# A state-space mixer with an MLP gate on one core: rows of the second half are stored early and gated products added in DRAM by accumulating DMAs

## The chip, the core and the metric

The kernel runs on one core of a Trainium2 chip. The core has five engines that run side by side, each in its own order: PE (matrix products), DVE (elementwise work on vectors), ACT (functions of one operand), POOL (some elementwise work early on, near the end an issuer of DMAs alone) and SP (an issuer of DMAs alone). ACT can issue DMAs too. The metric is the device time in microseconds (us) of one execution. Before the change it is 1081.44 us, the median of three runs (1080.97 to 1081.83).

## What is computed

The input `u` has 2048 tokens of 576 features. Each token is normalized; a long convolution along the tokens gives `s`, a two-layer network on each token gives `g`, and the output is the input plus their product:

```
xn  = layernorm(u)
s   = ssm_conv(xn)                      # a convolution of length 2048 per feature, by transforms
h   = gelu(xn @ w1 + b1)                # 576 -> 4608
g   = silu(h @ w2 + b2)                 # 4608 -> 576
out = u + s * g                         # float32
```

## The kernel before

**Tiling.** Tokens are cut into 16 tiles of 128. The tiles 0 to 7 are called the first half here, 8 to 15 the second. The hidden width of 4608 is cut into 12 groups of 384. A *slot* is one group for one block of four tiles: layer 1 (`layer1`, L519) makes three blocks of 128 hidden rows for 512 tokens, `hidden` turns them into a high part `hh` and a low part `hl` (L552, L555, L558), and layer 2 (`layer2`, L577) multiplies them with `w2` for four tiles, called j = 0 to 3. Each product is formed from three matmuls (high by high, low by high, high by low). After each tile of a slot DVE adds the PSUM result to the running sum `acc` (`add`, L585). There are 48 slots, PE works through them without a break, and the convolution's work is threaded in between.

**The end.** The last two slots finish tiles 8 to 11 and 12 to 15. As each tile's `acc` is complete, `finish` (L644) is called for it. For tiles 8 to 11 the gate is formed with tanh: ACT makes tanh(z/2) (L653), DVE multiplies `s` by z (L660) and by (1 + tanh) (L664). For tiles 12 to 15 it is formed with silu on ACT (L653) and one product on DVE (L658). Then `total` adds the product to the input row (L668) and stores the tile's sum with two DMAs of 64 rows each (L671), on SP; for tiles 14 and 15 the second of the two goes through ACT. The last tile, 15, is done in two halves of 288 columns: layer 2 writes its second half to another PSUM buffer (`cv`) so that the first half can be finished while PE still works.

**Where the rows come from.** `last_x` (L630) loads the input rows of tiles 8 to 15 on SP into freed table memory (named `w` and `v` in the trace), `last_s` (L636) loads their `s` into the freed buffer `A2` (named `A`). Both happen well ahead of the end. `combine_load` and `combine` (L613, L621) do the same for tiles 0 to 7 on POOL's queue, from stored gates: three loads, two DVE operations (L624, L625) and stores (L628). Their last set, tiles 6 and 7 in columns 384 to 576, falls between the two last slots. The buffers `row` (four of them) are shared by these loads and by ACT's gate (L653).

**What sets the order.** A planner (`Order`) keeps a modelled clock for each engine and traces the steps of many work lines in the order that its costs give; the traced order is then pinned on each engine. `finish` returns such steps, `need` names what a step must wait for in that model. Semaphore waits between engines follow from the data: an instruction waits for whoever wrote what it reads or reads what it overwrites. An engine that waits holds up what is queued behind it. A DMA also waits, on its issuing engine, for the DMA eight places earlier of its kind.

Of the kernel before, what the change touches and what calls it, by code (L numbers as in the profile page):

```python
# [13 lines left out]
OP = mybir.AluOpType  # L14
# [3 lines left out]
L, D, N, F = 2048, 576, 128, 4608  # L18
# [24 lines left out]
def dve(n):  # L43
    return 0.075 + 0.00104 * n
# [163 lines left out]
def step(eng, dur, fn, need=(), mark=None, cv=0, at=0.0, late=0.0, tbl=None, by=1e9):  # L208
    return dict(eng=eng, dur=dur, fn=fn, need=tuple(need), mark=mark, cv=cv, at=at, late=late, tbl=tbl, by=by)
# [3 lines left out]
def mixer_kernel(ctx, tc, u, log_a_real, a_imag, c_real, c_imag, log_dt, d_skip, w1, b1, w2, b2,  # L213
                 f1, f2, g2, g1, tvals, ident, out, parts=("mlp", "s4d")):
    nc = tc.nc
# [9 lines left out]
    def dram(ap_of, offset, ap):  # L225
        return bass.AP(tensor=ap_of.tensor, offset=ap_of.offset + offset, ap=ap)
# [97 lines left out]
    acc = sb.tile([P, 8, D], F32, name="acc")  # L324
# [283 lines left out]
    XS = {}  # L608

    def rows_at(t, b, c0, c1):  # L610
        return [dram(t, (b + 16 * y) * D + c0, [[32 * D, 64], [1, c1 - c0]]) for y in range(2)]
# [24 lines left out]
    def last_s(k):  # L636

        m = A2F[:, k * D:(k + 1) * D]
        nc.sync.dma_start(m, s_s[:, 8 + k, :])
        XS[8 + k] = (TM[k], m)  # L640

    TM = []

    def finish(b, c0, c1, silu, end):  # L644

        c = slice(c0, c1)
        z = acc[:, b - 8, c]
        n = c1 - c0
        T = []

        def act_z():
            T.append(sb.tile([P, D], F32, name="row", bufs=NROW)[:, c])
            nc.scalar.activation(T[0], z, AF.Silu if silu else AF.Tanh, scale=1.0 if silu else 0.5)  # L653

        def mul():
            s = XS[b][1][:, c]
            if silu:
                nc.vector.scalar_tensor_tensor(s, s, 2.0, T[0], op0=OP.mult, op1=OP.mult)  # L658
            else:
                nc.vector.tensor_mul(s, s, z)  # L660

        def mul2():
            s = XS[b][1][:, c]
            nc.vector.scalar_tensor_tensor(s, T[0], 1.0, s, op0=OP.add, op1=OP.mult)  # L664

        def total():
            x, s = XS[b]
            nc.vector.tensor_add(x[:, c], x[:, c], s[:, c])  # L668
            for y, o in enumerate(rows_at(out, b, c.start, c.stop)):
                queue = nc.scalar if end and y else nc.sync  # L670
                queue.dma_start(o, x[64 * y:64 * y + 64, c])  # L671
        st = [step("ACT", act(n), act_z, tbl="silu" if silu else "gelu"), step("DVE", dve(n), mul)]
        if not silu:
            st.append(step("DVE", dve(n), mul2))
        return st + [step("DVE", dve(n), total)]


    def params():
# [426 lines left out]
    NSLOT = 4 * NG  # L1105
    od = Order(tc, nc)
    od.pinned = True
    el, wl2, wl, nl2, pl, pl2, pl3, pl4, pl5, nl, ml, ml2, xl, wx, c3, c2, c1, kl, tl, sl, vl, gl, fl, f2l = [od.line() for _ in range(24)]
# [260 lines left out]
    for k in range(4):  # L1369
        gl["steps"].append(step("POOL", 5.0, lambda k=k: part.update({k: load_g2(k)}), mark=("g2", k),  # L1370
                                need=[("g2c", k - 1)] if k else []))
# [112 lines left out]
    for slot in range(NSLOT):  # L1484
        turn[0] = slot + 1
        n, g, tb = SEQ[slot]
        change = slot + 1 < NSLOT and SEQ[slot + 1][0] != n
        final = slot >= NSLOT - 2
        for pos in range(NPOS):
            if pos < G:  # L1490
                need = wmark(n, 1) + [("x", tb)]
                if pos == 0:
                    if slot in (mid, mid + 1):
                        x_ready(tb)
                    od.force(lambda: all(m in od.marks for m in need))

                    if slot in (3, 2 * NG + 1):
                        od.marks["x", tb] -= 2.3
                cell = []
                od.unit(lambda: cell.extend([layer1(g, tb, pos)] if slot else first_layer1(pos)),  # L1500
                        L1 if slot else L1 * (22, 6, 14)[pos] / 14, need)
                look_ahead(pos)
                for k, (a, b, c) in enumerate(cell, pos + 1 - len(cell)):
                    by = hidden_by(pos, k)
                    od.urgent.append((od.t["PE"], [step("ACT", 0.62, a, tbl="gelu", by=by[0]),
                                                   step("ACT", act(TB), b, by=by[1]),
                                                   step("DVE", dve(TB), c, mark=("h", slot, k), by=by[2])]))
                od.advance(od.t["PE"])
                if pos == G - 1 and change:
                    weigh_in(1)  # L1510
            else:
                j, terms, last, hid = l2_terms(pos - G)
                need = [wmark(n, 2)[i] for i in hid] + [("h", slot, i) for i in hid]
                if pos == G:

                    pe_turns()
                od.force(lambda: all(m in od.marks for m in need))
                if max(od.marks[m] for m in need) > od.t["PE"] + 0.3:
                    pe_turns(any_time=True)
                cell = []  # L1520
                halves = slot == NSLOT - 1 and j == 3
                od.unit(lambda: cell.append(layer2(g, tb, j, terms, last, halves)), LEN[pos], need)
                look_ahead(pos)
                if last or halves:
                    add = cell[0]
                    dh, k = (terms[0][1], 1) if halves else (0, 2)
                    done = ("acc", slot, j, dh)
                    chain = [step("DVE", dve(288 * k), lambda: add(dh, k), mark=done, by=add_by(pos, j))]
                    if final:
                        b = 8 + 4 * tb + j  # L1530
                        x = el if slot < NSLOT - 1 else od.line()
                        st = finish(b, dh * 288, (dh + k) * 288, slot == NSLOT - 1, slot == NSLOT - 1 and j > 1)
                        st[0]["need"] = (done, ("s8", b - 8))
                        x["steps"] += st
                    elif slot in GATE:
                        for d in range(2):
                            one, two = gate_store(4 * tb + j, d)
                            by = od.t["PE"] + 5.0
                            chain += [step("ACT", act(288), one, tbl="gelu", by=by), step("DVE", dve(288), two, by=by)]
                    od.urgent.append((od.t["PE"], chain))  # L1540
                if pos == NPOS - 1 and change:
                    weigh_in(2)
            for f in LATER.get((slot, pos), ()):
                f()
            od.advance(od.t["PE"])
            pe_turns(all_lines=pos in (0, 1, G + 1, G + 3, G + 5, NPOS - 1))
# [55 lines left out]
```

## Time and profile before

| | us |
|---|---|
| median of three runs | 1081.44 |
| profiled execution, its own time | 1081.68 |
| its span, first to last instruction | 1079.9 |
| PE busy (99% of the span) | 1070.8 |
| DVE busy (88%) | 955.2 |
| ACT busy (61%) | 662.2 |
| POOL busy (20%) | 211.0 |

Times in the views count from the span's start. The span is 1.8 us shorter than the execution's own time; that part lies outside of what the profile shows. The granted clock of PE is 0.998 over the span. A row of the timeline gives the start, the duration, the engine and its line, the operation, what it writes and reads, and in brackets the engine's idle time before it with what ended it. "Landing" of a DMA is the time from the start of its issue until its completion reaches the semaphore.

### The profile page before, as it was taken

The page shows a single profiled execution, that of the slowest core. Times are in us where ns is not written, and L with a number is a line of the kernel's source. Part 1 is how long each engine was busy: PE and PEld are TensorE (multiplying, and loading weights), DVE is VectorE, ACT ScalarE, POOL GpSimd, SP SyncE. Part 2 cuts the span into 40 slices and gives each one's busy share as a digit, 9 for nine tenths or more (in the row PEclk, how much of TensorE's full clock was granted, in tenths as well). Part 3 has the DMA queues.
Part 4 walks back from the last instruction along what each step waited for, and adds up shares of the span by engine and source line. Part 5 has one row for each costly group of instructions (what it writes and reads, how often), then busy time and mean ns, then how long its engine had stood idle before and what let it go on. Part 6 is the DMA issues. An engine that isn't in the chain of part 4 may idle for free.

```text
span 1079.9 us, 27247 instructions
## 1 busy us (share of the span) xinstructions
PE 1070.8 (99%) x11471; PEld 932.4 (86%) x11471; DVE 955.2 (88%) x1535; ACT 662.2 (61%) x985; POOL 211.0 (20%) x304
## 2 busy tenths in 40 slices
PE   9999999999999999999999999999999999999997
PEld 7989899888888888888888887898888888888896
DVE  7789878999999999999999999999999997668367
ACT  6656768877658575686657657566667655234233
POOL 5669433111100020000200002000200013011231
PEclk9999999999999999999999999999999999999999
DMA  7885456643224141457322244133322436343434
GB/s 233 236 261 184 145 180 213 197 109 131 65 76 120 30 128 52 107 148 147 89 62 77 65 85 118 32 107 51 103 59 85 125 60 229 98 132 98 128 117 121
DMA packets 138570, 129.71 MB, mean 120 GB/s; under 512 B 88636, under 2 KB 109216, under 8 KB 137424
## 3 DMA queue, kind: packets, MB, share of 16 engines
q1 hardware_dynamic: 121792, 78.31, 26.8%
q0 software_dynamic: 15904, 48.70, 14.6%
q8 instruction: 90, 1.47, 0.6%
q10 hardware_dynamic: 752, 0.97, 0.3%
q14 instruction: 32, 0.26, 0.1%
HBM read 98.50 MB, written 35.19 MB: 124 GB/s over the span
## 4 chain that ended last, share of the span: by engine, by line
PE 96%; DVE 3%; issue 1%; ACT 0%; POOL 0%; ACTq 0%; DVEq 0%; POOLq 0%
PE mxb L577 21%; PE mxa L577 21%; PE mxa L519 21%; PE mxb L519 20%; PE cv L881 3%; PE cv L991 3%; PE cv L1044 2%; PE cv L953 2%; PE cv L1071 1%; PE mxa L1132 1%; DVE w2l L496 0%; PE mxa L534 0%; DVE pr L720 0%; DVE hl L558 0%; DVE A L658 0%
## 5 line engine op out<-in xcount | busy, mean ns | idle before, releaser
L577 PE MATMUL mxa<-w2h,hh 128*128 128x288 f32 x573 | 171.3, 299 | 0.3 <-DVE acc L585 0.3
L577 PE MATMUL mxb<-w2h,hh 128*128 128x288 f32 x576 | 171.6, 298 | 0.0
L577 PE MATMUL mxb<-w2h,hl 128*128 128x288 f32 x576 | 170.2, 296 | 0.0
L577 PE MATMUL mxb<-w2l,hh 128*128 128x288 f32 x576 | 169.5, 294 | 0.0
L577 PE MATMUL mxa<-w2h,hl 128*128 128x288 f32 x573 | 169.4, 296 | 0.2 <-DVE hl L558 0.2
L577 PE MATMUL mxa<-w2l,hh 128*128 128x288 f32 x573 | 168.7, 294 | 0.0
L558 DVE TENSOR_TENSOR hl<-h,hh 128x512 fp32r<-128x512 f32 x144 | 99.2, 690 | 65.2 <-ACT hh L555 64.7
L552 ACT ACTIVATE h<-mxa,b1t 128x512 f32<-128x512 f32 x73 | 50.3, 690 | 120.8 <-PE mxa L519 119.8
L781 POOL DMA_DIRECT2D par<-par_s x36 | 27.4, 762 | 480.4 <-DVE mg L824 436.4
L577 PEld LDWEIGHTS mxa<-w2h,hh 128*128 128x128 f32 x573 | 107.6, 188 | 9.8 <-issue 4.7
L577 PEld LDWEIGHTS mxb<-w2h,hh 128*128 128x128 f32 x576 | 108.1, 188 | 7.7 <-issue 3.0
L577 PEld LDWEIGHTS mxb<-w2l,hh 128*128 128x128 f32 x576 | 108.1, 188 | 0.6
L577 PEld LDWEIGHTS mxb<-w2h,hl 128*128 128x128 f32 x576 | 108.1, 188 | 0.4 <-DVE hl L558 0.2
L577 PEld LDWEIGHTS mxa<-w2h,hl 128*128 128x128 f32 x573 | 107.5, 188 | 0.6 <-DVE hl L558 0.6
L577 PEld LDWEIGHTS mxa<-w2l,hh 128*128 128x128 f32 x573 | 107.6, 188 | 0.5
L552 ACT ACTIVATE h<-mxb,b1t 128x512 f32<-128x512 f32 x71 | 49.0, 690 | 74.0 <-PE mxb L519 73.3
L555 ACT ACTIVATE hh<-h 128x512 fp32r<-128x512 f32 x144 | 91.2, 634 | 4.2
L585 DVE TENSOR_TENSOR acc<-mxa,acc 128x576 f32<-128x576 f32 x88 | 65.7, 746 | 21.3 <-PE mxa L577 20.8
L519 PE MATMUL mxa<-XH,w1h 128*128 128x512 f32 x284 | 78.9, 400 | 0.0
L519 PE MATMUL mxb<-XH,w1h 128*128 128x512 f32 x280 | 77.5, 398 | 0.0
L519 PE MATMUL mxa<-XL,w1h 128*128 128x512 f32 x284 | 76.2, 390 | 0.0
L519 PE MATMUL mxa<-XH,w1l 128*128 128x512 f32 x284 | 76.0, 389 | 0.0
(239 smaller groups left out, 2450.9 us busy)
## 6 DMA issues: line engine op xcount, KB each, us to landing
raw<-in_B_w_dram SPq DMA_DIRECT2D x75, 288.0 KB, 3.3
raw<-in_B_w_dram SPq DMA_DIRECT2D x100, 192.0 KB, 3.4
par_s<-A POOLq DMA_DIRECT2D x8, 1080.0 KB, 5.2
par<-par_s POOLq DMA_DIRECT2D x36, 240.0 KB, 3.4
f2t<-f2q SPq DMA_DIRECT2D x24, 256.0 KB, 3.5
raw<-in_B_w_dram SPq DMA_DIRECT2D x50, 96.0 KB, 3.6
u_s<-in_A_u_dram POOLq DMA_DIRECT2D x16, 288.0 KB, 4.8
xc<-xn_s SPq DMA_DIRECT2D x48, 96.0 KB, 3.8
```

Source lines behind the costliest of these rows:

```text
L519: nc.tensor.matmul(q, a, b, start=j == 0, stop=j == len(ops) - 1)
L552: nc.scalar.activation(t, q, AF.Gelu_apprx_tanh, bias=b1t[:, g * G + i:g * G + i + 1], scale=1.0)
L555: LAST[0] = nc.scalar.activation(hh[:, i], t, AF.Copy)
L558: nc.vector.tensor_sub(hl[:, i], t, hh[:, i].bitcast(F32))
L577: nc.tensor.matmul(q[:, dh, :288], a[:, i, c], b[:, i, d], start=i == 0 and k == 0, stop=i == G - 1 and k == 2)
L585: nc.vector.tensor_add(o, q[:, dh:dh + n, :288], b if first else o)
L781: nc.gpsimd.dma_start(PAR[b].rearrange("p (g i) k -> p g (i k)", g=4), dram(par_s, (b // 6 * CH + b % 6 * 4) * NPAR, [[D * NPAR, P], [24 * ...
L881: nc.tensor.matmul(q[32 * g:32 * g + 32, i // 2, i % 2 * 64:i % 2 * 64 + 64], U[:, ri, 4 * g + i, :], v[:, ri, 4 * g + i, :], start=ri == ...
L953: nc.tensor.matmul(Q1ST[i, x][g // 2][64 * f:64 * f + 64, g % 2].rearrange(order), f1t[r].rearrange("p s k -> p (s k)"), rhs(r, f), start= ...
L991: nc.tensor.matmul(Q[i][32 * q:32 * q + 32, f, 2 * ri:2 * ri + 2], m[r, 4 * i + q, 32 * ri:32 * ri + 32], A2[r, 4 * p + 2 * i + q // 2, :, ...
L1044: nc.tensor.matmul(QI[q // 2][64 * f:64 * f + 64, q % 2, i], MAT["g2t", p + i // 2][r, i % 2, ri], YS[p + i // 2][0][r, i % 2, ri, f], sta ...
L1071: nc.tensor.matmul(Q[f][32 * e:32 * e + 32, t], g1t[r], A2[r, k:k + 2, 1].rearrange("p i d r -> p i r d"), start=True, stop=True, skip_gro ...
```

## The change

```diff
--- before.py
+++ after.py
@@ -638,6 +638,9 @@
         m = A2F[:, k * D:(k + 1) * D]
         nc.sync.dma_start(m, s_s[:, 8 + k, :])
         XS[8 + k] = (TM[k], m)
+        if k < 7:
+            for y, o in enumerate(rows_at(out, 8 + k, 0, D)):
+                nc.sync.dma_start(o, TM[k][64 * y:64 * y + 64])
 
     TM = []
 
@@ -652,27 +655,34 @@
             T.append(sb.tile([P, D], F32, name="row", bufs=NROW)[:, c])
             nc.scalar.activation(T[0], z, AF.Silu if silu else AF.Tanh, scale=1.0 if silu else 0.5)
 
+        def product(a, k, op, b2):
+            x, s = XS[b]
+            o = s[:, c] if end else x[:, c]
+            nc.vector.scalar_tensor_tensor(o, a, k, b2, op0=op, op1=OP.mult)
+            if not end:
+                for y, r in enumerate(rows_at(out, b, c0, c1)):
+                    nc.gpsimd.dma_start(r, o[64 * y:64 * y + 64], accum_op=OP.add)
+
         def mul():
             s = XS[b][1][:, c]
             if silu:
-                nc.vector.scalar_tensor_tensor(s, s, 2.0, T[0], op0=OP.mult, op1=OP.mult)
+                product(s, 2.0, OP.mult, T[0])
             else:
                 nc.vector.tensor_mul(s, s, z)
 
         def mul2():
-            s = XS[b][1][:, c]
-            nc.vector.scalar_tensor_tensor(s, T[0], 1.0, s, op0=OP.add, op1=OP.mult)
+            product(T[0], 1.0, OP.add, XS[b][1][:, c])
 
         def total():
             x, s = XS[b]
             nc.vector.tensor_add(x[:, c], x[:, c], s[:, c])
             for y, o in enumerate(rows_at(out, b, c.start, c.stop)):
-                queue = nc.scalar if end and y else nc.sync
+                queue = nc.scalar if c1 == D and y else nc.sync
                 queue.dma_start(o, x[64 * y:64 * y + 64, c])
         st = [step("ACT", act(n), act_z, tbl="silu" if silu else "gelu"), step("DVE", dve(n), mul)]
         if not silu:
             st.append(step("DVE", dve(n), mul2))
-        return st + [step("DVE", dve(n), total)]
+        return st + [step("DVE", dve(n), total)] * end
 
 
     def params():
@@ -1529,8 +1539,10 @@
                     if final:
                         b = 8 + 4 * tb + j
                         x = el if slot < NSLOT - 1 else od.line()
-                        st = finish(b, dh * 288, (dh + k) * 288, slot == NSLOT - 1, slot == NSLOT - 1 and j > 1)
+                        st = finish(b, dh * 288, (dh + k) * 288, slot == NSLOT - 1, slot == NSLOT - 1 and j == 3)
                         st[0]["need"] = (done, ("s8", b - 8))
+                        if halves and not dh:
+                            st[1]["need"] = (("acc", slot, j, 1),)
                         x["steps"] += st
                     elif slot in GATE:
                         for d in range(2):
```

For tiles 8 to 14 the input rows, once loaded, are stored to `out` at once, with two DMAs per tile on SP that directly follow the load of that tile's `s` in SP's order. The gate's last product is then written over the loaded row tile and added to `out` by two DMAs per tile that POOL issues with an accumulating operation; the DVE sum and the SP stores (or SP and ACT) at the end go away for these seven tiles. The last tile keeps its sums and plain stores, and only the very last of its four stores is on ACT. In the model, the first half's product of the last tile also waits for the second half's `acc`.

At the program's end, DVE stood as follows before. `acc<-mxb_12986`, `acc<-mxa_13013` and `acc<-cv_13027` are the sums of tile 14 and of the two halves of tile 15; `w` and `v` are the input rows, `row` the gates, `A2` is `s`.

```order
L668 TENSOR_TENSOR w_11310<-w_11310,A2_81 128x576
L658 SCALAR_TENSOR_TENSOR A2_81<-A2_81,row_12997 128x576
L585 TENSOR_TENSOR acc_87<-mxb_12986,acc_87 128x576
L668 TENSOR_TENSOR w_11310<-w_11310,A2_81 128x576
L585 TENSOR_TENSOR acc_87<-mxa_13013,acc_87 128x288
L658 SCALAR_TENSOR_TENSOR A2_81<-A2_81,row_13037 128x576
L585 TENSOR_TENSOR acc_87<-cv_13027,acc_87 128x288
L668 TENSOR_TENSOR v_11311<-v_11311,A2_81 128x576
L658 SCALAR_TENSOR_TENSOR A2_81<-A2_81,row_13040 128x288
L668 TENSOR_TENSOR v_11311<-v_11311,A2_81 128x288
L658 SCALAR_TENSOR_TENSOR A2_81<-A2_81,row_13046 128x288
L668 TENSOR_TENSOR v_11311<-v_11311,A2_81 128x288
```

And with the change, where `acc<-mxb_12996`, `acc<-mxa_13024` and `acc<-cv_13037` are the same three sums:

```order
L585 TENSOR_TENSOR acc_87<-mxa_12961,acc_87 128x576
L661 SCALAR_TENSOR_TENSOR w_11310<-A2_81,row_12993 128x576
L661 SCALAR_TENSOR_TENSOR w_11310<-A2_81,row_13009 128x576
L585 TENSOR_TENSOR acc_87<-mxb_12996,acc_87 128x576
L585 TENSOR_TENSOR acc_87<-mxa_13024,acc_87 128x288
L661 SCALAR_TENSOR_TENSOR v_11311<-A2_81,row_13034 128x576
L585 TENSOR_TENSOR acc_87<-cv_13037,acc_87 128x288
L661 SCALAR_TENSOR_TENSOR A2_81<-A2_81,row_13050 128x288
L678 TENSOR_TENSOR v_11311<-v_11311,A2_81 128x288
L661 SCALAR_TENSOR_TENSOR A2_81<-A2_81,row_13054 128x288
L678 TENSOR_TENSOR v_11311<-v_11311,A2_81 128x288
```

The full-width sums of tiles 12 to 14 (L668, 576 wide) are gone, and `acc<-cv` of the last half stands directly behind tile 14's product, ahead of the first half's product.

ACT's end before, with the gates of tiles 12, 13, 14 and of tile 15's halves:

```order
L653 ACTIVATE row_12983<-acc_87 128x576
L653 ACTIVATE row_12997<-acc_87 128x576
L653 ACTIVATE row_13037<-acc_87 128x576
L653 ACTIVATE row_13040<-acc_87 128x288
L671 DMA out_0_dram<-v_11311 64x576
L653 ACTIVATE row_13046<-acc_87 128x288
L671 DMA out_0_dram<-v_11311 64x288 x2
```

With the change:

```order
L656 ACTIVATE row_12993<-acc_87 128x576
L656 ACTIVATE row_13009<-acc_87 128x576
L656 ACTIVATE row_13034<-acc_87 128x576
L656 ACTIVATE row_13050<-acc_87 128x288
L656 ACTIVATE row_13054<-acc_87 128x288
L681 DMA out_0_dram<-v_11311 64x288
```

The DMA that stood between the two half gates of tile 15 is gone, and only one store is left.

POOL's end before, from the second to last set of first-half stores on:

```order
L628 DMA out_0_dram<-row_12711 64x192 x6
L616 DMA row_12873<-u_s_65 128x2x192
L617 DMA row_12874<-s_s_64 128x2x192
L618 DMA row_12875<-g_s_68 128x2x192
L628 DMA out_0_dram<-row_12873 64x192 x4
```

With the change, L664 being the accumulating DMAs, `w_11309` and `w_11310` holding tiles 8 to 10 and 11 to 13, `v_11311` tiles 14 and 15:

```order
L628 DMA out_0_dram<-row_12725 64x192 x6
L664 DMA out_0_dram<-w_11309 64x576 x4
L616 DMA row_12890<-u_s_65 128x2x192
L617 DMA row_12891<-s_s_64 128x2x192
L618 DMA row_12892<-g_s_68 128x2x192
L664 DMA out_0_dram<-w_11309 64x576 x2
L664 DMA out_0_dram<-w_11310 64x576 x2
L628 DMA out_0_dram<-row_12890 64x192 x4
L664 DMA out_0_dram<-w_11310 64x576 x4
L664 DMA out_0_dram<-v_11311 64x576 x2
```

Four accumulating DMAs (tiles 8 and 9) now stand ahead of the loads for the last first-half set, four (tiles 10 and 11) ahead of that set's stores, and six (tiles 12 to 14) behind them at the queue's end. On SP, each load of `s` (L639) for tiles 8 to 14 is now followed by two stores of rows, among the last three loads of `w2` (L459), which before had one load of `s` between them; the order on PE is the same.

## The prediction

> **What bounds the kernel now.** I read the page's busy times first, then its chain of work, then the stretches at the end, then the timelines of the engines there.
>
> ```profile
> PE 1070.8 (99%) x11471; PEld 932.4 (86%) x11471; DVE 955.2 (88%) x1535; ACT 662.2 (61%) x985; POOL 211.0 (20%) x304
> PE 96%; DVE 3%; issue 1%; ACT 0%; POOL 0%; ACTq 0%; DVEq 0%; POOLq 0%
> 1060.00:1066.00 6.00, 6.00 (x38) 5.46 (x37) 4.10 (x8) 3.93 (x5) 0.00 (x0) 1.00 0.42 98
> 1072.80:1079.90 7.10, 0.00 (x0) 0.00 (x0) 3.29 (x7) 0.83 (x2) 0.00 (x0) 0.71 0.49 125
> ```
>
> PE is busy for 99% of the span and makes 96% of the chain. The stretch from 1060 to 1066 (columns: length, then busy us of PE, weight load, DVE, ACT, POOL, clock, DMA) shows it full in the last slot as well. The change leaves PE's instructions and their order alone, so as long as nobody makes PE wait, it can only alter what comes behind PE's last matmul, the 7.1 us of the last row. PE's last matmul and DVE's work around it:
>
> ```profile
> 1072.48 0.29 PE L577 MATMUL cv<-w2h,hl 128*128 128x288 f32 x1
> ...
> 1068.73 0.75 DVE L658 SCALAR_TENSOR_TENSOR A<-A,row 128x576 f32<-128x576 f32 x1
> 1069.52 0.76 DVE L668 TENSOR_TENSOR w<-w,A 128x576 f32<-128x576 f32 x1
> 1070.19 0.75 DVE L658 SCALAR_TENSOR_TENSOR A<-A,row 128x576 f32<-128x576 f32 x1
> 1070.86 0.75 DVE L585 TENSOR_TENSOR acc<-mxb,acc 128x576 f32<-128x576 f32 x1
> 1071.53 0.75 DVE L668 TENSOR_TENSOR w<-w,A 128x576 f32<-128x576 f32 x1
> 1072.20 0.45 DVE L585 TENSOR_TENSOR acc<-mxa,acc 128x288 f32<-128x288 f32 x1
> 1072.56 0.75 DVE L658 SCALAR_TENSOR_TENSOR A<-A,row 128x576 f32<-128x576 f32 x1
> 1073.23 0.45 DVE L585 TENSOR_TENSOR acc<-cv,acc 128x288 f32<-128x288 f32 x1
> 1073.60 0.75 DVE L668 TENSOR_TENSOR v<-v,A 128x576 f32<-128x576 f32 x1
> 1074.26 0.45 DVE L658 SCALAR_TENSOR_TENSOR A<-A,row 128x288 f32<-128x288 f32 x1
> 1074.75 0.46 DVE L668 TENSOR_TENSOR v<-v,A 128x288 f32<-128x288 f32 x1
> 1075.60 0.46 DVE L658 SCALAR_TENSOR_TENSOR A<-A,row 128x288 f32<-128x288 f32 x1 [0.39 <-ACT row L653]
> 1076.09 0.46 DVE L668 TENSOR_TENSOR v<-v,A 128x288 f32<-128x288 f32 x1
> ```
>
> PE ends at 1072.48 + 0.29 = 1072.77, but DVE adds the last half (`acc<-cv`) only at 1073.23: it is 0.46 behind, with two full-width totals (L668 at 1069.52 and 1071.53) in its way. Then ACT:
>
> ```profile
> 1068.85 0.69 ACT L653 ACTIVATE row<-acc 128x576 f32<-128x576 f32 x1 [0.91 <-DVE acc L585]
> ...
> 1074.38 0.54 ACTq L671 DMA_DIRECT2D out_dram<-v  x1
> 1075.12 0.45 ACT L653 ACTIVATE row<-acc 128x288 f32<-128x288 f32 x1 [1.93 <-DVE A L658]
> ```
>
> The last gate could start at 1073.23 + 0.45 = 1073.68. It starts at 1075.12, since ACT's queue holds tile 14's store ahead of it, and that waits for the total that DVE ends at 1074.35. So the tail holds two losses: 0.46 us on DVE and 1.44 us on ACT. Behind them come the last product, the last total (its end 1076.55) and the stores:
>
> ```profile
> L671 ACTq DMA_DIRECT2D out_dram<-v x1: 498/498/498, 1076.6 to 1076.6; - x1
> DMA to landing us min/median/max: 2.0/2.1/2.2
> ...
> L1598 SPq DRAIN  x3: 7/7/7, 1079.1 to 1079.4; - x3
> ```
>
> The last two stores are issued at 1076.6 on SP and ACT and land 2.0 and 2.2 later, the later one at 1078.8; SP, which waits for all DMAs at the end, lets go at 1079.1, and the span ends at 1079.9. From last landing to the end: 1.1 us.
>
> **The tail rebuilt, step by step.** Durations are those of the rows above. Independent neighbours on DVE start 0.67 apart (1070.19 to 1070.86) at full width and 0.37 (1073.23 to 1073.60) after a half; dependent halves start 0.49 apart (1075.60 to 1076.09). An engine takes up another's result 0.03 to 0.06 later. Tile 12's product stays at 1068.73. Without its total, tile 13's product starts at 1069.6 in place of 1070.19, when its gate (1068.85 + 0.69) is ready. Tile 14's sum starts when PE is done with it, about 1070.45; its gate on ACT runs 1071.23 to 1071.92; the first half's sum comes with PE at 1071.62, its gate ends at 1072.55; tile 14's product runs 1072.05 to 1072.80. The last sum now starts with PE's end, 1072.81, ends at 1073.26; the last gate, with no DMA in ACT's queue ahead, runs 1073.29 to 1073.74. Meanwhile DVE makes the first half's product at 1073.18 and its total at 1073.67. The last product starts at 1074.04, the last total at 1074.53, ending 1074.99 where it was 1076.55: **1.56 us earlier**.
>
> Not all of it arrives. The first half's two stores are now both on SP:
>
> ```profile
> 1072.31 1.11 SPq L671 DMA_DIRECT2D out_dram<-w  x2
> ```
>
> A pair holds SP for 1.11 us. From 1074.16 it ends at 1075.3, so SP's last store starts about 1075.35, not 1075.02; it lands 2.0 later at 1077.35 (ACT's lands 2.2 after 1075.02, or 2.5 at worst: not later than 1077.5). Before, SP's landed at 1078.6. The gain on this path is **1.2 us**. All seven removed totals (seven times 0.75) otherwise free only DVE time that waits for PE anyway, as the chain's 96% says: nothing beyond the two in the tail.
>
> **The added accumulating DMAs.** POOL takes up a DVE result late:
>
> ```profile
> 1065.88 0.56 DVE L625 TENSOR_TENSOR row<-row 128x384 f32<-128x384 f32 x1
> ...
> 1066.73 2.13 POOL L628 DMA_DIRECT2D out_dram<-row  x4 [10.92 <-DVE row L625]
> ```
>
> 0.30 us after DVE's end (1066.43), and 0.53 us for each DMA of 64 rows. Tile 12's pair then issues from 1069.8, tile 13's from 1070.9 to 1072.0, tile 14's at 1073.1 and 1073.65, ending 1074.2. No row shows an accumulating DMA, which has to read `out` as well as write it. The nearest:
>
> ```profile
> g_s<-acc POOLq DMA_DIRECT2D x8, 288.0 KB, 2.4
> out_dram<-row POOLq DMA_DIRECT2D x16, 48.0 KB, 1.9
> u_s<-in_A_u_dram POOLq DMA_DIRECT2D x16, 288.0 KB, 4.8
> row<-u_s POOLq DMA_DIRECT2D x9, 192.0 KB, 3.4
> ```
>
> A plain store of POOL, 288 KB, lands after 2.4 us: the lower bound for these 144 KB. A copy of 288 KB within DRAM, which reads and writes there, takes 4.8: the upper bound. A load of 192 KB takes 3.4, about 1 us above a store, and I take that 1 us for the read: 2.4 + 1.0 = 3.4, so the last one lands at 1077.05, ahead of SP's 1077.35: hidden by the last tile's own chain. At 4.8 it lands at 1078.45 and, with 1.1 us behind it, ends the span at 1079.55: the gain shrinks to 0.35.
>
> The Trainium skill speaks to this (Collectives: The Full Stack, "The bandwidth ceiling: the fold count and why AG ≠ RS ≠ AR"): an add inside the DMA engine costs a second read, so it moves at half the rate, and nothing for the add itself. With the fit of DMA: Bandwidth & Descriptors ("Anatomy of one DMA — SWDGE (gpsimd) path"), 2.0 us plus bytes over 436 GB/s, 147,456 bytes read twice would land after an estimated 2.7 us; no run here shows it yet, and by it the sum would stay and the case in which the landing holds the end would lose its ground.
>
> POOL also has a closing step of its own:
>
> ```profile
> L1598 POOLq DRAIN  x3: 46/103/3731, 1068.1 to 1079.6; - x3
> ```
>
> It ends 3.73 after 1068.08, at 1071.8: 2.95 after POOL's last issue ended (1066.73 + 2.13 = 1068.86). Counted so, it now ends at 1077.15, free. Its DMAs had landed by about 1070.2 (1.9 after the last issue's start); if it follows the landing by 1.65, it ends at 1078.7 and releases the end 0.4 before the old 1079.1. I take the first, since ACT's queue shows no such tie; the second goes to a rival.
>
> **Earlier work that is moved.** The fourteen early stores cost SP issue time among the last weight loads:
>
> ```profile
> 1017.04 2.69 SPq L639 DMA_DIRECT2D A<-s_s  x5
> 1028.22 0.81 SPq L459 DMA_DIRECT2D raw<-in_B_w_dram  x2
> 1030.28 0.33 SPq L459 DMA_DIRECT2D raw<-in_B_w_dram  x1
> 1034.70 1.84 ACT L499 ACTIVATE w2h<-raw 128x576 fp32r<-128x576 f32 x3 [6.09 <-PE mxa L577]
> ```
>
> Ten of them, with five loads, sit between 1017.04 and the load at 1028.22, which is released by DVE: about 15 times 0.55, or 8.3 us of 11.2, with some waiting for the DMA eight earlier. One pair (1.11) then precedes the third `w2` load, which moves from 1030.28 to about 1030.8, lands some 3.3 later at 1034.1, and is needed for the third of ACT's splits, from 1035.9: 1.8 us of cover. On POOL, four accumulating DMAs precede the loads for the last first-half set:
>
> ```profile
> 1053.08 0.73 POOL L616 DMA_DIRECT2D row<-u_s  x1
> 1055.09 0.72 POOL L618 DMA_DIRECT2D row<-g_s  x1 [0.56 <-issue]
> 1065.29 0.55 DVE L624 TENSOR_TENSOR row<-row 128x384 f32<-128x384 f32 x1
> ```
>
> Tile 9's product is ready near 1054, so the loads issue from 1055.2 instead of 1053.08; the last lands near 1057 + 4 = 1061, and DVE wants it at 1065.3: 4 us of cover. ACT's gates of tiles 8 to 11 now stand together ahead of the next gelu, which may come one gate (0.69 us) later at worst; two more layer-1 blocks of PE stand before its result is wanted. These edits cost nothing; without the covers each would show as PE idle, one for one.
>
> **The sum.** Span 1079.9 - 1.2 = 1078.7, and 1081.68 - 1.2 = 1080.5 for the profiled execution, which lies 0.24 above the median. On the median's scale: 1081.44 - 1.2 = 1080.24, rounded to **1080.3 us**.
>
> **The rivals.**
> - *POOL's end holds the end*: the accumulating landing at 4.8, or the closing step tied to it. The lower bound of 0.35 to 0.4 us gained, up to a wash: 1081.0 to 1081.8. For it: the read of DRAM is unmeasured, and the closing step's length is unexplained. Against it: the landing has 0.3 us to spare at 3.4.
> - *Slower, by POOL's issue*: an accumulating DMA that holds POOL longer than 0.53. Six follow tile 12's product from 1069.8, so the last starts at 1069.8 + 5t and lands 3.4 later; it passes the old last landing (1078.8) at t = 1.1. At t = 1.5 the end is 1.9 us later (1083.3), at t = 2 it is 4.4 later (1085.8). For it: nothing shows such a DMA. Against it: 64 rows cost 0.53 and the 256 rows of the load at 1053.08 cost 0.73, so the number of rows hardly matters.
> - *PE is made to wait* in the last two slots, by slow accumulating DMAs ahead of the first-half loads or by traffic on the weights: beyond the 4 or 1.8 us of cover, each microsecond adds one; 2 to 5 us, 1083 to 1086.
> - *The tail doesn't shorten*, because ACT's last gate waits for the first-half stores that free its `row` buffer. They issue by 1068.86 and land near 1070.2, 3 us ahead of 1073.3: only with POOL held up, which is the second rival.
>
> **How the numbers follow.** The forecast gets 0.66, the first rival 0.18, the second 0.11, the third 0.05; the last has no share of its own. The forecast's own range is 1079.7 to 1081.0 (the runs of before spread by 0.4 either way). The range to give goes from 1079.7 to 1083.0: it takes in the first rival and the milder part of the second. A change of 0.2%, 2.16 us, is about what a measurement of this kernel can tell from none. A gain of that size would have to come from more than the two losses in the tail, whose 1.9 us are already an upper bound: 0.03. Slower by that needs t near 1.5 or a held PE: 0.11. Within 0.2%: 0.86.
>
> **What would show it.** `acc<-cv` within 0.1 us of PE's end; the last gate directly behind it; the last total ending 2.2 us after PE (before 3.8); seven fewer L668; accumulating issues of 0.53 and landings between 2.4 and 4.8; POOL's closing step over before SP's. Wrong it would be by idle time of PE after 1015, by POOL issues over 1 us each, or by a last landing that is POOL's.

## The result and the profile after

The change makes the kernel **slower**: 1083.34 us (median of 19 runs, 1082.58 to 1084.61) against 1081.41 us for the kernel before in the same rounds (19 runs, 1080.83 to 1082.35). The ratio is 1.0019 with a 95% interval of 1.0012 to 1.0026, so the loss is 1.3 to 2.8 us, where a gain of about 1.2 was forecast.

The profiled execution of the change took 1084.61 us, the highest of its runs, with a span of 1082.8. PE's last matmul ends 0.68 us later than before, at 1073.16 + 0.29 = 1073.45. That shift stands almost whole (0.60) at DVE's first sum already, 26 us into the span and ahead of everything the change moves (every engine's order is the same up to 1018 us), and PE has no wait that it had not before; it belongs to the execution and not to the change. All tails are therefore compared from PE's end on. The tail was 7.13 us (1072.77 to 1079.9) and is now **9.38** (1073.45 to 1082.83): 2.25 more, about the difference of the medians (1.93).

The end of the kernel after, in the timelines of PE, DVE and ACT:

```profile
1073.16 0.29 PE L577 MATMUL cv<-w2h,hl 128*128 128x288 f32 x1
...
1072.67 0.75 DVE L661 SCALAR_TENSOR_TENSOR v<-A,row 128x576 f32<-128x576 f32 x1
1073.49 0.46 DVE L585 TENSOR_TENSOR acc<-cv,acc 128x288 f32<-128x288 f32 x1
...
1075.21 0.46 DVE L678 TENSOR_TENSOR v<-v,A 128x288 f32<-128x288 f32 x1
...
1073.98 0.44 ACT L656 ACTIVATE row<-acc 128x288 f32<-128x288 f32 x1 [0.68 <-DVE acc L585]
```

The last sum follows PE by 0.04 us (0.46 before), the last gate starts 0.53 behind PE's end (2.35 before), and the last total ends 2.22 behind it (3.77 before). The arithmetic is done 1.55 us earlier, as forecast. What follows is DMAs. The stretches behind PE's end (length, busy us of PE, weight load, DVE, ACT, POOL, then clock, share of the DMA engines and GB/s):

```profile
1073.40:1076.00 2.60, 0.05 (x1) 0.00 (x0) 2.13 (x6) 0.44 (x1) 2.16 (x3) 0.88 0.98 133
1076.00:1080.40 4.40, 0.00 (x0) 0.00 (x0) 0.00 (x0) 0.00 (x0) 0.00 (x0) 0.50 0.72 149
1080.40:1082.80 2.40, 0.00 (x0) 0.00 (x0) 0.00 (x0) 0.00 (x0) 0.00 (x0) 0.50 0.00 0
```

While DVE still works, the 16 DMA engines are at 98%, and for 4.4 us after it they are all that works. Then comes a stretch of 2.4 us in which no DMA moves and the kernel still doesn't end. The two rows of DMAs at the end (accumulating ones on POOL, tile 15's plain stores), and the engines' closing steps, each view with count, shortest, median and longest in ns, then first and last start:

```profile
L664 POOL DMA_DIRECT2D out_dram<-w x12: 852/1518/3018, 1053.8 to 1072.3; - x12
L664 POOL DMA_DIRECT2D out_dram<-v x2: 996/1144/1292, 1073.7 to 1074.3; - x2
DMA to landing us min/median/max: 3.2/5.1/6.6
...
L681 SPq DMA_DIRECT2D out_dram<-v x3: 467/609/681, 1074.8 to 1076.1; - x3
DMA to landing us min/median/max: 4.0/4.6/4.8
...
L1610 POOLq DRAIN  x3: 46/103/7850, 1074.2 to 1082.6; - x3
L1610 SPq DRAIN  x3: 7/7/7, 1081.0 to 1082.3; - x3
```

Three things are to be read from this. An accumulating DMA with none ahead of it lands after 3.2 to 3.3 us; the median of the fourteen is 5.1 and the slowest takes 6.6. Tile 15's plain stores, which took 2.0 to 2.5 before, now take 4.0 to 4.8, and SP's closing step starts at 1081.0, 7.56 behind PE's end (6.30 before). And POOL's closing step, from 1074.19, lasts 7.85 us: it ends at 1082.04, 8.59 behind PE's end, and only then does the program end, 0.79 later.

The six accumulating DMAs of tiles 12 to 14, from their issues and landings in the trace (us from PE's end):

| | 1 | 2 | 3 | 4 | 5 | 6 |
|---|---|---|---|---|---|---|
| issue | -2.99 | -2.43 | -1.88 | -1.17 | +0.27 | +0.81 |
| landing after | 3.33 | 4.50 | 4.69 | 5.42 | 4.78 | 5.71 |
| landed | +0.34 | +2.07 | +2.80 | +4.25 | +5.04 | +6.53 |

They land (6.53 - 0.34) / 5 = 1.24 us apart on average, while they are issued (0.81 + 2.99) / 5 = 0.76 apart (0.54 to 0.71 within a tile): a queue. The trace's packets show it on the DMA engines. A row of 2304 bytes of such a DMA holds its engine for 195 ns at the least and 264 in the mean (896 packets); plain rows of that size, in the stores of the kernel before, take 91 at the least and 148 in the mean. The six DMAs bring 24 rows to each of the 16 engines, in all 6.3 us of work for each, and they are issued within 3.8 us.

### The profile page after: what moved, and what is told of

Read it like the earlier page. It is cut to its first block, busy times and chain, and to the rows that moved or that the text cites. A ratio compares the mean times of both kernels' runs of the same rounds, so it can differ in the third digit from the quotient of the medians.

```text
span 1082.8 us, 27264 instructions
## 1 busy us (share of the span) xinstructions
PE 1071.4 (99%) x11471; PEld 932.6 (86%) x11471; DVE 950.8 (88%) x1528; ACT 661.2 (61%) x985; POOL 222.7 (21%) x318
## 4 chain that ended last, share of the span: by engine, by line
PE 94%; DVE 3%; DMA 1%; issue 0%; ACT 0%; DVEq 0%; ACTq 0%
PE mxb L577 21%; PE mxa L577 21%; PE mxa L519 21%; PE mxb L519 20%; PE cv L891 3%; PE cv L1001 3%; PE cv L1054 2%; PE cv L963 2%; PE cv L1081 1%; DMA raw<-in_B_w_dram 0%; DVE hl L558 0%; DVE w2l L496 0%; PE mxa L534 0%; DVE pr L730 0%; DVE acc L585 0%
## 5 line engine op out<-in xcount | busy, mean ns | idle before, releaser
L552 ACT ACTIVATE h<-mxa,b1t 128x512 f32<-128x512 f32 x73 | 50.1, 687 | 120.6 <-PE mxa L519 120.4
```

Of the source, the lines that this page charges most:

```text
L552: nc.scalar.activation(t, q, AF.Gelu_apprx_tanh, bias=b1t[:, g * G + i:g * G + i + 1], scale=1.0)
```

## The experiments

The theories: **A**, the accumulating DMAs cost more than they free, because their rows queue on the DMA engines, crowd tile 15's stores, and POOL's closing step follows the last landing. The rivals: the new order and queues cost the time, or the early moves do, or the closing step follows POOL's issues, whatever the DMAs do. All numbers of tails below are us behind PE's end, read from the timelines and landings of each run's trace. The kernels of one set ran beside the kernel before on the same chip.

### First set (before: 1081.32 us)

**`plain_pool`**: the accumulating DMAs become plain stores. The input rows are left out of tiles 8 to 14.

```diff
-                    nc.gpsimd.dma_start(r, o[64 * y:64 * y + 64], accum_op=OP.add)
+                    nc.gpsimd.dma_start(r, o[64 * y:64 * y + 64])
```

> The changed kernel with plain POOL stores in place of the accumulating ones (the same queue, sizes and order; the input rows of tiles 8 to 14 are thereby left out of the output). Theory 1 (accumulating DMAs are served one after another at about 1.25 us each, since each packet takes 196 ns where a plain one takes 93, and POOL's closing step waits for the last landing plus about 2 us): landings fall to 2.4 us, the closing step ends before SP's, the end is the forecast's: 1.2 us below before. Theory 2 (the closing step is work of POOL that grows with the number of its late DMAs, 6.5 us after the last issue for six): still about 1.9 us above before. Theory 3 (any six extra DMAs crowd tile 15's stores): stores still land after more than 3.5 us and the time is 0.5 to 1.9 us above before.

Measured 1080.67 us, ratio 0.9994 (0.9985 to 1.0002), tail 6.42. Its issues in the last 14 us (KB of each, median us to landing) and its closing step:

```profile
out_dram<-w POOLq DMA_DIRECT2D x4, 144.0 KB, 2.7
out_dram<-v SPq DMA_DIRECT2D x3, 72.0 KB, 2.2
out_dram<-v POOLq DMA_DIRECT2D x2, 144.0 KB, 2.6
...
L1611 POOLq DRAIN  x3: 46/103/4873, 1072.4 to 1077.8; - x3
L1611 SPq DRAIN  x3: 7/7/7, 1077.0 to 1077.6; - x3
```

With the same issues, order and early stores but without the add, the tail is 9.38 - 6.42 = 2.96 us shorter than with it, and tile 15's stores land after 2.2. The add inside the DMAs is what costs. The early moves and as many issues of POOL are in this run too, so neither of them makes the loss. One thing else changes with it: the plain stores go out in packets of two rows, 4608 bytes, of 296 ns each in the mean. That is 148 ns for each row, as in the single-row packets of the kernel before, so the size of the packets is not what makes the difference. The median is 0.65 us below before (the interval includes 1), not the 1.2 of the first theory: POOL's closing step still ends last, at +5.63, 2.06 behind POOL's last landing (+3.57) and 0.35 behind SP's (+5.28).

**`acc_14`**, **`acc_8_11`** and **`order_only`** use the accumulating DMAs for tile 14 alone, for tiles 8 to 11, and for none. The other tiles keep sums and stores as before, but in the change's order and queues.

```diff
+ACC = (14,)        # acc_8_11: (8, 9, 10, 11); order_only: ()
...
-        if k < 7:
+        if 8 + k in ACC:
...
-                queue = nc.scalar if c1 == D and y else nc.sync
+                queue = nc.scalar if b == 15 and c1 == D and y else nc.sync
...
-                        st = finish(b, dh * 288, (dh + k) * 288, slot == NSLOT - 1, slot == NSLOT - 1 and j == 3)
+                        st = finish(b, dh * 288, (dh + k) * 288, slot == NSLOT - 1, b not in ACC)
```

> Only tile 14 accumulates; tiles 8 to 13 have their sums on DVE and plain stores on SP. Theory 1: the two accumulating DMAs issue about 0.9 us behind PE's end and 0.55 later, land 3.3 and about 4 us after that, the closing step ends 2 us later: 0.8 to 1.2 us above before. Theory 2 (two late DMAs, a third of the closing step's 6.5): the closing step ends in time, 0.3 to 0.8 us below before. Theory 3: tile 15's stores are crowded by two DMAs in place of six, no more than 0.3 us above before.

> Only tiles 8 to 11 accumulate, all eight DMAs more than 5 us ahead of PE's end; tiles 12 to 14 as in the kernel with the order alone. Theories 1 and 2: the closing step follows the first-half stores near 1072 and binds nothing; the time equals that of the order alone, within 0.3 us. A rival (accumulating DMAs ahead of the first-half loads make DVE and then PE wait): 1 us or more above the order alone, with idle time of PE in the last slots.

> No accumulating DMAs and no early stores: all tiles keep their sums; only the end's order and queues are those of the change (tile 14's stores both on SP, no DMA of ACT ahead of the last gate). If the tail is as in the prediction's working, the last gate starts 0.05 us behind the last sum (1.4 us earlier), but DVE's full sum of tile 14 stays in the way and the last total ends only 0.5 us earlier; SP's queue now holds five stores behind each other (tile 14's pair 1.1 us, tile 15's first pair 1.1 us), so that SP's last store starts when it did: 0 to 0.4 us below before. Rival (the whole forecast gain comes from ACT's queue): 1.2 us below before.

Measured: `acc_14` 1082.15 us, 1.0008 (0.9999 to 1.0017), tail 7.91; `acc_8_11` 1082.19, 1.0007 (0.9999 to 1.0016), tail 7.96; `order_only` 1081.84, 1.0005 (0.9996 to 1.0014), tail 7.64. Each of the three intervals includes 1, so the tails carry the reading. `order_only` ends its last total at +3.29, 0.48 earlier than before, and its tail is yet 0.51 longer. SP's queue at its end:

```profile
1069.84 3.11 SPq L682 DMA_DIRECT2D out_dram<-w  x4
1073.91 3.20 SPq L682 DMA_DIRECT2D out_dram<-v  x5
```

Five stores stand on SP where there were three (tile 14's second one and the first half's second one have left ACT), so the last goes out at +4.08 where it was +3.80. So this order and these queues alone lose about half a microsecond of tail, where the expectation was a gain of 0 to 0.4. It is no part of the change's loss: with the change tile 14 has no plain stores, SP's queue holds three again, and `plain_pool`, with the same three, has a shorter tail than before. In `acc_14` two accumulating DMAs at the very end are enough to let POOL's closing step end last: landed at +5.55, ended at +7.12, against SP's +6.78. In `acc_8_11` the accumulating DMAs are over well ahead of the end. Its tail is 0.32 longer than that of `order_only`, but SP's closing step comes at +6.83 against +6.81; nearly all of the rest arises behind it, in the program's last steps.

### Second set (before: 1080.77 us)

**`one_dma`**: one accumulating DMA for each tile instead of two, with as many rows and bytes.

```diff
-                for y, r in enumerate(rows_at(out, b, c0, c1)):
-                    nc.gpsimd.dma_start(r, o[64 * y:64 * y + 64], accum_op=OP.add)
+                nc.gpsimd.dma_start(dram(out, b * D + c0, [[16 * D, 2], [32 * D, 64], [1, c1 - c0]]), o, accum_op=OP.add)
```

> The changed kernel with one accumulating DMA of 128 rows per tile in place of two of 64. Theory A (the DMA engines are held per packet: a row of 2304 bytes costs them 196 ns and more when it is added): the same rows, so the last accumulating landing stays 6 to 6.6 us behind PE's end and the time within 0.4 us of the changed kernel's. Theory B (each accumulating DMA costs a fixed 0.5 us or so, its first packets take 400 to 840 ns): three fewer DMAs in the tail, the last landing about 1.5 us earlier, the time 1 to 1.5 us below the changed kernel's.

Measured 1105.43 us, ratio 1.0227 (1.0213 to 1.0241): both expectations missed. Landings, PE's longest wait (us in total, times, longest) and the closing steps:

```profile
L664 POOL DMA_DIRECT2D out_dram<-w x6: 1412/1812/2893, 1053.1 to 1078.2; - x6
DMA to landing us min/median/max: 15.0/17.3/20.6
...
PE mxb L578 <- DVE acc L586: 7.1, 1, 7.1
...
L1610 POOLq DRAIN  x3: 46/173/21052, 1082.7 to 1104.6; - x3
```

The first of them lands after 15.0 us. That is 64 rows at 196 ns, 12.5 us, and 2.5 beside it, as if the 128 rows went through two DMA engines and not 16. The packets agree: from 14.0 to 18.5 us behind PE's end, where the last of these DMAs runs alone, the DMA share of the stretch is 0.12 of 16 engines, or 1.9 of them. The Trainium skill has this (DMA: Bandwidth & Descriptors, "Rules for kernel authors"): an outermost dimension shorter than 16 confines a DMA to as many engines, and the destination here begins with a dimension of 2. So this run doesn't tell rows from DMAs, but it shows two other things. The loads of the last first-half set stand behind two such DMAs (tiles 8 and 9), land 16.6 to 17.0 us after their issue, and PE waits 7.1 us: the prediction's third rival, at work. And POOL's closing step ends 1.77 us after the last landing, 19.7 after the last issue: it follows **the landing**.

**`acc_12_14`**: accumulating for tiles 12 to 14 only (`ACC = (12, 13, 14)`, edits as in `acc_14`).

> Only tiles 12 to 14 accumulate, tiles 8 to 11 keep sums and plain stores. If the loss is made in the tail alone, by the six late accumulating DMAs and the closing step that follows the last of them: the tail behind PE's end is the changed kernel's, 9.4 us, and the time 1.5 to 2.2 us above before. Rival (the eight earlier ones and the early stores take part, by traffic or by the wait for the DMA eight places ahead): the tail is shorter by 0.5 us or more.

Measured 1082.65 us, ratio 1.0017 (1.0007 to 1.0026), tail 8.79, last landing +6.27. The six at the end make 8.79 - 7.13 = 1.66 of the 2.25 us. The eight earlier ones and their early stores add about 0.6, by one trace of each kernel: the last landing comes 0.26 later with them and POOL's closing step stands 0.33 further behind it. So the rival, 0.5 us or more, came true beside the main expectation; the times don't tell the two kernels apart.

**`order_fix`**: no accumulating DMAs; the change's order on DVE and ACT, but tile 14's second store stays on ACT and is issued behind the last gate instead of ahead of it.

```diff
-                queue = nc.scalar if c1 == D and y else nc.sync
-                queue.dma_start(o, x[64 * y:64 * y + 64, c])
+                queue = nc.scalar if b >= 14 and y else nc.sync
+                LATE.append((queue, o, x[64 * y:64 * y + 64, c]))
+            while len(LATE) > (b == 14):
+                q, o, i = LATE.pop(0)
+                q.dma_start(o, i)
```

> No accumulating DMAs, all sums on DVE; tile 14's second store stays on ACT but is issued behind the last gate, and tile 15's stores are spread over SP and ACT. Working: last gate 0.94 us behind PE's end as with the order alone, last total ending at 3.29 (before 3.77), the last stores of both queues start there and not at 4.1: the tail is 6.6 to 6.7 us (before 7.1, order alone 7.6), the time 0.3 to 0.5 us below before. Rival (the tail is bound by the landings of all five late stores, not by when the last one starts): 7.1 us or more.

Measured 1080.29 us, ratio 0.9995 (0.9986 to 1.0004), tail 6.67, as worked out. ACT at its end:

```profile
1073.08 0.44 ACT L657 ACTIVATE row<-acc 128x288 f32<-128x288 f32 x1 [0.53 <-DVE acc L586]
1073.74 2.24 ACTq L685 DMA_DIRECT2D out_dram<-v  x3
```

The last gate starts at +0.94 and all three of ACT's stores follow it. This takes the larger of the two losses that the prediction found in the tail (1.44 us on ACT) without any accumulating DMA: the tail is 0.46 shorter than before and 2.7 shorter than after. It is the fastest median of the kernels here that compute the whole output, though its interval against the kernel before includes 1, so the gain is read from the tail and not shown by the times.

**`pool_tot`**: `order_fix`, with the full-width totals of tiles 12 to 14 on POOL.

```diff
-            nc.vector.tensor_add(x[:, c], x[:, c], s[:, c])
+            (nc.gpsimd if b in ONPOOL else nc.vector).tensor_add(x[:, c], x[:, c], s[:, c])
```

> As the one with the stores spread, and the full sums of tiles 12 to 14 are made by POOL (an elementwise add of 128x384 took it 1.02 us, so about 1.5 us each) in place of DVE or of an accumulating DMA; plain stores on SP and ACT. Working: the last gate 0.53 us behind PE's end, the last total ending at 2.2 as in the changed kernel; POOL's sum of tile 14 ends near 1.8, its stores and tile 15's follow each other on each queue, the last start near 2.9, the tail is 6.1 to 6.4 us, the time 0.7 to 1.0 us below before. Rival (POOL's reading slows DVE's operations with two operands in SBUF, or POOL's closing step follows late): the last total ends after 2.6, the tail is 6.9 us or more.

Measured 1081.03 us, ratio 1.0002 (0.9993 to 1.0011), tail 7.40, the last total ending at +4.03: worse than `order_fix`, as the rival had it. Its timelines of DVE and POOL:

```profile
1069.66 0.76 DVE L587 TENSOR_TENSOR acc<-mxb,acc 128x576 f32<-128x576 f32 x1
1070.85 0.46 DVE L587 TENSOR_TENSOR acc<-mxa,acc 128x288 f32<-128x288 f32 x1 [0.42 <-PE mxa L579]
1071.22 1.61 DVE L663 SCALAR_TENSOR_TENSOR A<-A,row 128x576 f32<-128x576 f32 x1
1072.76 0.44 DVE L587 TENSOR_TENSOR acc<-cv,acc 128x288 f32<-128x288 f32 x1
1073.13 1.55 DVE L663 SCALAR_TENSOR_TENSOR A<-A,row 128x288 f32<-128x288 f32 x1
...
1068.79 3.43 POOL L680 TENSOR_TENSOR w<-w,A 128x576 f32<-128x576 f32 x2 [0.71 <-DVE A L663]
1072.97 1.40 POOL L680 TENSOR_TENSOR v<-v,A 128x576 f32<-128x576 f32 x1 [0.75 <-issue]
```

Beside POOL's sums DVE's products take 1.61 us for 0.75 (full width) and 1.55 for 0.45 (half width). The sums of `acc`, which take one operand from PSUM, keep their times: 0.76 at 1069.66 and 0.46 at 1070.85, both while POOL's sums run. POOL's closing step here ends at +5.32, 2.95 behind POOL's last sum, though its last DMA landed 7.9 earlier: the step takes time of its own also where it has no landing to wait for.

### Third set (before: 1080.82 us)

What does an accumulating DMA pay for: its rows, its bytes, or itself?

**`split4`**: four accumulating DMAs of 32 rows for each tile in place of two of 64.

```diff
-                for y, r in enumerate(rows_at(out, b, c0, c1)):
-                    nc.gpsimd.dma_start(r, o[64 * y:64 * y + 64], accum_op=OP.add)
+                for y in range(4):
+                    r = dram(out, (b + 16 * (y // 2) + 1024 * (y % 2)) * D + c0, [[32 * D, 32], [1, c1 - c0]])
+                    nc.gpsimd.dma_start(r, o[32 * y:32 * y + 32], accum_op=OP.add)
```

> Four accumulating DMAs of 32 rows for each of tiles 8 to 14, in place of two of 64: the same rows of 2304 bytes, twice the DMAs and twice POOL's issues. Theory A (the price is per row: an accumulating row holds its DMA engine 196 to 261 ns against about 90 for a plain one, so the rows of tiles 12 to 14 queue): the last accumulating landing stays about 6.1 to 6.6 us behind PE's end, and the time from PE's end to the span's end stays at 9.0 to 9.6 us (9.38 with two). Theory B (each accumulating DMA has a fixed time of its own in the queue, 0.5 us or more, besides its rows): six more DMAs at the end put the last landing at +9 or later and the end at 11 us or more behind PE's.

**`half_rows`**: only the first 288 columns are added for tiles 8 to 14; the product's other half is left out of the output.

```diff
-                for y, r in enumerate(rows_at(out, b, c0, c1)):
-                    nc.gpsimd.dma_start(r, o[64 * y:64 * y + 64], accum_op=OP.add)
+                for y, r in enumerate(rows_at(out, b, c0, c0 + 288)):
+                    nc.gpsimd.dma_start(r, o[64 * y:64 * y + 64, :288], accum_op=OP.add)
```

> The accumulating DMAs of tiles 8 to 14 add only the first 288 of 576 columns (the other half of the product is left out of the output): as many DMAs and as many rows, of 1152 bytes instead of 2304. Theory A (an accumulating row costs by its bytes): 98 to 130 ns a row, the last accumulating landing about 3.7 us behind PE's end, and 6.6 to 7.0 us from PE's end to the span's end. Theory B (an accumulating row costs a fixed time, whatever its bytes): nothing changes, the last landing at about +6.5 us and the end at about 9.4 us.

Measured: `split4` 1086.67 us, ratio 1.0058 (1.0035 to 1.0081), tail 13.01, last landing +8.74; `half_rows` 1080.79, ratio 0.9999 (0.9987 to 1.0010), tail 7.19, last landing +4.34. The DMA queues of the last 14 us (packets, MB, share of 16 engines), first of the kernel after, then of `half_rows`:

```profile
q0 software_dynamic: 577, 1.03, 50.1%
q1 hardware_dynamic: 240, 0.22, 5.3%
```

```profile
q0 software_dynamic: 480, 0.44, 28.9%
q1 hardware_dynamic: 240, 0.22, 5.5%
```

POOL's queue (q0, which in the kernel after also holds a few first-half stores) takes 28.9 against 50.1% of the DMA engines' time. By the packets, the accumulating rows of tiles 12 to 14 alone take 3.9 us of each engine with half the bytes and 6.3 with all, and the shortest rows go from 195 to 111 ns. So the bytes count for the greater part (theory A in `half_rows`, though its tail is 0.2 above its range and its last landing 0.6 above the 3.7 expected). But they are not all: in `split4` the same rows in twice as many DMAs land 0.79 us apart, (8.74 - 0.09) / 11, and not 0.62 as half of 1.24 would be. If the spacing is a fixed part and a part by rows, 1.24 = f + 4r and 0.79 = f + 2r (rows for each of 16 engines) give r = 0.225 us and f = 0.34 us, an estimate from two spacings. What the fixed part is stays open: in `split4` the DMA engines are not full, 82% busy in the first 4 us behind PE's end against 98% in the kernel after. Tile 15's stores go with that: three of the four can be timed in `split4`, and they land after 2.1 to 3.2 us, earlier than in the kernel after, though more accumulating DMAs stand in the queue. Theory B, a fixed time for each DMA, holds beside A; its landing came 0.3 below what it expected, its end as expected:

```profile
L1612 POOLq DRAIN  x3: 46/103/9419, 1075.9 to 1085.9; - x3
```

POOL's closing step ends at +12.22, 3.48 behind the last landing instead of 2.06. Beyond the landing it takes longer where POOL has issued many: 1.64 us with none of these DMAs, 1.57 with two, 1.73 with six, 2.06 with fourteen (the kernel after, `plain_pool` and `half_rows` alike) and 3.48 with twenty-eight. `acc_8_11`, with eight, doesn't fit (2.27, though there it doesn't hold the end). What it does in that time no run shows.

## Why the prediction was wrong, step by step

- **Only the tail can change; PE is not touched.** Right. PE's waits are those of before, and the early stores and the moved loads did no harm to it. The cover was needed, though: in `one_dma` the held loads cost PE 7.1 us.
- **The tail rebuilt.** Right to a few hundredths: last gate 0.53 behind PE, last total ending at +2.22 (forecast 1074.99 - 1072.77 = 2.22).
- **POOL's issues, 0.53 each.** Right where they matter: they start 0.54 to 0.71 apart within a tile, so the second rival's mechanism (a slow issue) is not what happened. The rows of 0.85 to 3.0 us are over the 1 us that was named as a sign of being wrong, but they overlap and do not hold POOL that long.
- **The accumulating landing.** The step that failed: "I take that 1 us for the read: 2.4 + 1.0 = 3.4, so the last one lands at 1077.05, ahead of SP's 1077.35: hidden by the last tile's own chain." The 3.4 is right for one alone (3.2 to 3.3). But it was given to the sixth of a row of six, as if none stood before it. They land 1.24 us apart and are issued 0.76 apart, so the later ones wait; the last takes 5.71 and lands at +6.53, against a forecast of +4.28. Even the upper bound of 4.8 was a bound for one DMA alone.
- **The last tile's stores, 2.0 to 2.2.** Wrong for the same reason: they meet DMA engines that the queue keeps full (98% busy) and land after 4.0 to 4.8. SP's closing step comes at +7.56 where it was +6.30, so even if POOL had not been waited for, the tail would have been about 0.8 longer than that, 8.4, more than the 7.13 of before. `plain_pool` puts them back to 2.2.
- **POOL's closing step.** "I take the first, since ACT's queue shows no such tie": the wrong choice. It ends 1.57 to 2.27 us behind the last landing in the runs with up to fourteen of these DMAs (`pool_tot` apart, where POOL's sums come later than its last landing) and 1.77 behind it in `one_dma`, where the last issue is 19.7 us away. The profile of before gave 1.65 for that reading, and 2.95 for the one that was taken, and could not tell them apart; the second was priced and left to a rival. It adds 8.59 - 7.56 = 1.03 us to the tail behind SP's step.
- **The first rival** held both mechanisms, but each alone and with the landing of a single DMA, so that its worst was a wash. Together, with the queue, they make the loss. The range reached 1083.0 for the wrong reason and still fell 0.3 short.
- **The half rate.** The Trainium skill gives it for an add in the DMA engine (Collectives: The Full Stack, "The bandwidth ceiling: the fold count and why AG ≠ RS ≠ AR"). The shortest packets agree (195 against 91 ns, and 111 against 48 to 51 for rows of 1152 bytes); the means of the longer rows stand at 264 against 148, 1.8 times. The estimate of 2.7 us for a landing, made from the fit of the Trainium skill's DMA: Bandwidth & Descriptors ("Anatomy of one DMA — SWDGE (gpsimd) path"), lies 0.5 below the DMAs with none ahead of them and 3.0 below the last of the queue. A rate at half is a matter for a queue and not for one landing, and that is how it should have been used.

The account of the tail: the change without its add gains (`plain_pool`: 9.38 - 2.96 = 6.42 against 7.13, so 0.7), and the add in the DMAs costs 2.96; the sum is the 2.25 us by which the tail is longer. The forecast's 5.93 with everything hidden was out of reach in any case: without the add, POOL's closing step and stores of up to 2.4 us leave 6.42.

## What to carry to other kernels

A DMA's landing when it is alone says nothing of six in a row: multiply rows per DMA engine by the time of a row (here 4 by 264 ns, about 1.06 us), and where that is above the distance of the issues (0.76 us), expect a queue, and late landings for the plain stores beside it. Before work is put on an engine's DMA queue at a program's end, look at what that engine's closing step waits for. And where an edit mixes a new order with a new mechanism, try the order alone: here, with tile 14's second store moved behind the last gate, it shortens the tail (`order_fix`, 6.67 us for 7.13) without the price.

## What was not expected of the hardware

- An accumulating row of 2304 bytes holds its DMA engine for 264 ns in the mean, a plain one for 148 (195 against 91 at the least), and a DMA of 64 of them takes about 1.24 us in a queue, of which some 0.34 (estimate) don't depend on its rows.
- POOL's closing step ends 1.6 to 2.3 us after POOL's last DMA has landed where that comes last on POOL, 3.48 after twenty-eight of them; SP's starts 0.2 to 0.6 us behind the last landing of all (0.24 before the change, 0.51 after it, 0.63 in `split4`).
- A destination of 2 by 64 rows kept two DMA engines busy (1.9 by the packets), not 16: 15.0 to 20.6 us for one DMA and 24.7 us more for the kernel (1105.43 - 1080.77).
- POOL's elementwise sums stretch DVE's products beside them, all operands in SBUF, from 0.75 to 1.61 and from 0.45 to 1.55 us.
